# Bias loads over two iterations, shared-block copies on ScalarE, token weights pinned behind the attention

## The chip, the cores and the metric

The kernel runs on one core of a Trainium2 chip. The metric is the device time of one execution in microseconds, as the median of several runs. Five engines work side by side, each through its own instruction queue in order: TensorE (PE, with weight loads as PEld), VectorE (DVE), ScalarE (ACT), GpSimd (POOL) and SyncE (SP). In this kernel SP issues nearly all DMAs.

## The reference, cut to what matters

```python
scores = scale * q @ k.T + bias            # bias[h]: 576 x 576, the same for all 4 batches
attn = softmax(scores); x = attn @ v       # 4 batches, 8 heads, 576 tokens, 64 per head
gate_pre[t] = sum_k conv_w[k] * x[t-4+k]   # 5 taps along the tokens
x = (sigmoid(gate_pre) * (x @ w_val)) @ w_out
theta = x @ w_theta
y = w_tok_r @ (x * cos(theta)) + w_tok_i @ (x * sin(theta))
u = x + y
out = u + relu(u @ w_ch)
```

All inputs are 64-bit floats where they are weights: the kernel fetches the bits of a weight block and makes two 32-bit parts of it (high and low) on the engines.

## The kernel before, in words

**Stages.** First the bias of all heads is computed and stored to scratch in HBM (0 to about 60 us). Then the attention runs (to about 313 us), then the first module (gate and two products, to about 424 us), then the second (theta, the token product, the channel product).

**The attention** has 16 iterations: 4 pairs of heads, and for each pair 4 batches (`self.iters`). An iteration has 5 units `qt` 0 to 4: four blocks of 128 query tokens and a last one in which the 64 left tokens of both heads share one tile. One *step* `s` of the loop in `attention` works at once on three units: scores and softmax of unit `s` (`qk`, `soft`: a DVE instruction at L256 that adds the bias and takes the maximum, then the exponential on ACT at L259), the normalisation on POOL of unit `s-1` (`norm`), the transposes on PE of unit `s-2` (`tr`, `tr_mid`) with their copies out of PSUM (`tr_out`, `mid_out`, through `copy`, L279 on ACT and L281 on DVE), and products with v (`av_ops`, L358). The order of all these is written out by hand: the loop runs under `tc.manual_schedule()`, and each engine gets them in program order. "Shared blocks" are the transposes of `tr_mid` and the last unit: blocks in which two heads share a tile. `mid_out` copies them (tile `em`) on DVE; a letter pair in `EV` says which engine makes the two copies of `tr_out`.

**Beside it** run other pieces, also in that order. `load_bias(p, qt)` fetches the bias of a pair: for `qt` 0 to 3 two DMAs of 288 KB each into one of six `bias` slots (a pair takes four), for `qt` 4 two of 144 KB into one of two `biast` slots. Before, all five are issued in the five steps of the last batch of the pair ahead. `load_qkv(it + 2)` is issued in step 4 of each iteration. `WS` spreads the weight blocks of `w_val`, `w_out`, the convolution and `w_theta`: a block's fetch (`raw`) is issued at the end of step 2, ACT reads it first (L82) at the end of step 4 of the same iteration, and seven more stages follow over two iterations (DVE at L85, L91, L96, L101, then ACT L105 and POOL L108). In the last 16 steps hooks add the first chunk of the convolution, 20 DVE instructions (L469, L478), one a step.

**What the framework orders.** All that is traced outside the manual part is ordered by the framework: it puts each instruction where, by its own estimate, its engine is free, also among the attention's, and the compiled queues then run in that order. So it does with the nine blocks of token weights (`tokblock`, the same eight stages, with two `raw` slots and one `f64h` slot), which `pace` traces between the instructions of the first module, and with `prep`, the convolution of the next chunk. In the trace the fetches of the first three token blocks are issued at 249.5, 266.3 and 278.3 us, inside the attention.

**The first module** works on 8 chunks of 288 tokens: products with `w_val` (48 matmuls a chunk), the gate (`m1_gate`, DVE L509, then a high part on ACT at L63 and a low part on POOL at L65), products with `w_out` of the chunk before. The PSUM of its `gs` tiles and its `mm` tiles lies over that of the attention.

Of the kernel before, what the change touches and what calls it, by code (L numbers as in the profile page):

```python
# [13 lines left out]
AF = mybir.ActivationFunctionType  # L14
# [104 lines left out]
class Kernel:  # L119
# [124 lines left out]
    def soft(self, u, e):  # L244
        nc = self.nc
        it, qt = self.units[u]
        p, _ = self.iters[it]
        if e == 0:
            self.sh[it, qt] = (self.sm_p.tile([128, 2], F32, tag="sm", name="sm"),
                               self.e_p.tile([128, 2 * S], F32, tag="e", name="e"),  # L250
                               self.sm_p.tile([128, 2], F32, tag="mx", name="mx"))
        sm, et, mx = self.sh[it, qt]
        bt = self.bias_t[p, qt]
        ns = self.ns_p.tile([128, 2, HALF], F32, tag="ns", name="ns")
        bb = bt[:, e] if qt < 4 else bt
        nc.vector.tensor_tensor_reduce(  # L256
            out=ns, in0=self.s4[e][:, :, :HALF], in1=bb.rearrange("p (n j) -> p n j", n=2),
            op0=ALU.add, op1=ALU.min, scale=-0.125, scalar=BIG, accum_out=mx[:, e:e + 1])
        nc.scalar.activation(out=et[:, S * e:S * e + S], in_=ns.rearrange("p n j -> p (n j)"), func=AF.Exp,  # L259
                             scale=-1.0, bias=mx[:, e:e + 1], accum_out=sm[:, e:e + 1])  # L260

    def norm(self, u):
        nc = self.nc
# [52 lines left out]

    EV = ["ad", "ad", "aa", "ad", "ad"]

    def mid_out(self, u):
        qt = self.units[u][1]  # L320
        if qt not in (1, 4):
            return
        _, dst, _ = self.ets_dst(u)
        self.copy("d", dst[:, :256], self.po[0][:, 256:512])
        if qt == 4:
            for h in range(2):
                r = slice(64 * h, 64 * h + 64)
                self.copy("d", dst[r, 256:320], self.po[1][r, 384 + 64 * h:448 + 64 * h])

    def tr_out(self, u, eng):  # L330
        qt = self.units[u][1]
        dst, _, o = self.ets_dst(u)
        pt = self.pt[u]
        for h in range(2):
            if self.EV[qt][h] == eng:
                if qt < 4:
                    self.copy(eng, dst[:, o // 64 + h].rearrange("p k q -> p (k q)"), pt[h])
                else:
                    self.copy(eng, dst[:, 4, 4 * h:4 * h + 4].rearrange("p k q -> p (k q)"), pt[h][:, :256])

    def av_ops(self, it, ch):
        nc = self.nc
        p, b = self.iters[it]
        N = 256 + TT * ch
        et, em = self.ets.pop((it, ch))
        vm = self.qkv[it][2]
        po = self.po[ch]
        if ch == 0:
            self.xst[it] = self.xs_p.tile([128, S], F32, tag="xst", name="xst")
        xst = self.xst[it]  # L350

        def step(kb):
            for e in range(2):
                r = slice(64 * e, 64 * e + 64)
                out, rhs = po[r, :N], em[:, :N]
                if kb < 4:
                    out, rhs = out.rearrange("p (h q) -> p h q", q=64), et[:, :N // 64, 4 * e + kb]
                nc.tensor.matmul(out=out, lhsT=vm[:, kb, r], rhs=rhs, start=(kb == 0), stop=(kb == 4))  # L358

        def done():  # L360
            nc.scalar.activation(out=xst[:, 256 * ch:256 * ch + N], in_=po[:, :N], func=AF.Copy)
            if ch == 1:
                nc.sync.dma_start(out=self.x1d[b][:, p, :], in_=xst)

        return [lambda kb=kb: step(kb) for kb in range(5)] + [done]

# [1 line left out]

    WS = ((2, 0, 5, 2), (2, 1, 6, 2), (2, 2, 7, 2), (0, 2, 0, 2), (0, 4, 1, 2), (1, 2, 2, 1), (1, 4, 3, 0),
          (1, 4, 4, 1))  # L370

    AV = {2: (1, 1), 3: (0, 2), 4: (0, 3), 0: (1, 2), 1: (1, 2)}

    def attention(self, blocks, hooks):
# [5 lines left out]
        for s in range(NU + LT + 2):  # L380
# [2 lines left out]
            n = 0 if s >= NU else 2 if r < 4 else 1  # L383
            if s < NU:
                p, b = self.iters[it]
                if b == B - 1 and p + 1 < NP:
                    self.load_bias(p + 1, r)
                for e in range(2):
                    self.qk(s, e)
                if r == 4 and it + 2 < NI:  # L390
                    self.load_qkv(it + 2)
# [308 lines left out]
    def run(self):  # L700
# [11 lines left out]
        with ExitStack() as top:  # L712
# [15 lines left out]
            with ExitStack() as att:  # L728
# [5 lines left out]
                self.e_p = pool(att, "a_e", cfg["EB"], "right", **T)  # L734
                self.sm_p = pool(att, "a_sm", 6, "right", **T)
                blocks, hooks = [], {}
                attention = self.attention(blocks, hooks)
                ps_s = pool(att, "a_ps", 1, space=PSUM, **T)
                self.s4 = [ps_s.tile([128, 2, 512], F32, name=f"s{e}") for e in range(2)]
# [82 lines left out]
            with ExitStack() as m1:  # L822
# [7 lines left out]
                def pace():  # L830
                    slots[0] += 1
                    while todo and (total - len(todo)) * cfg["PC"] < slots[0] * total:
                        todo.pop(0)()

                def prep(c, m):
                    self.m1_conv(c, m)
                    self.m1_sig(c, m)

                NCH = 2 * B
                for c in range(NCH + 1):  # L840
                    for m in range(KC):
# [2 lines left out]
                        elif c < NCH:  # L844
                            self.m1_val(c, m)
                        if c + 1 < NCH:
                            prep(c + 1, m)
                        pace()
                    for m in range(KC):
                        if c == NCH and m in cfg["TH"]:  # L850
# [126 lines left out]
```

## Time and profile before

| | us |
|---|---|
| median of 3 runs | 646.0 (644.36 to 648.67) |
| the profiled execution | 651.17 |
| its span, first to last instruction | 649.4 |
| PE busy in it | 615.2 (95%) |
| DVE busy | 467.3 (72%) |
| ACT busy | 393.4 (61%) |
| POOL busy | 344.5 (53%) |

The mean granted TensorE clock is 0.978 of full speed. Busy shares are means over stages that differ, so the stages are read one by one below. "Busy" of PE is modelled: where it is full, PE is fed without a pause. Iterations of the attention are cut at the DVE instruction that reads a `biast` tile, once an iteration, or, to the same 0.1 us, at the issue of the next q load.

### The profile page before, as it was taken

To read this page: it belongs to the slowest core of one execution; us is meant where nothing else is said; L and a number is where in the kernel's file an instruction comes from. 1 tells how busy PE (TensorE), PEld (TensorE's weight loads), DVE (VectorE), ACT (ScalarE), POOL (GpSimd) and SP (SyncE) were. 2 spreads that over 40 slices of the span, in tenths; PEclk is the share of its full clock that TensorE was granted. 3 is DMA by queue.
4 is the path that set the end of the run, shared out by engine and by line. 5 is a ranking of instruction groups with operands and counts; after the bars stand their busy time and mean duration, and the time that the engine had idled before them with its cause. 6 is when DMAs were issued, how large, how long until landed. Compare 5 with 4: busy or idle time off the path is not lost.

```text
span 649.4 us, 14576 instructions
## 1 busy us (share of the span) xinstructions
PE 615.2 (95%) x5472; PEld 473.2 (73%) x5472; DVE 467.3 (72%) x1089; ACT 393.4 (61%) x851; POOL 344.5 (53%) x422
## 2 busy tenths in 40 slices
PE   6997999999999999989499999999999999999997
PEld 2333555555555555546399999988998999899997
DVE  7995788888887889976579999089987717516212
ACT  5995688788787877656457775388544613613010
POOL 5553567677676666656558875334484324025120
PEclk9998799999999999979799999999999999999999
DMA  7997549755964794431035661623224001200102
GB/s 184 304 312 206 157 127 229 203 150 165 259 177 128 190 256 130 141 92 56 19 110 158 213 173 49 236 70 98 66 74 153 18 1 69 79 1 28 46 1 73
DMA packets 49413, 84.39 MB, mean 130 GB/s; under 512 B 6960, under 2 KB 27568, under 8 KB 48832
## 3 DMA queue, kind: packets, MB, share of 16 engines
q1 hardware_dynamic: 49168, 83.12, 43.9%
q8 instruction: 43, 0.70, 0.5%
q10 hardware_dynamic: 144, 0.30, 0.1%
q14 instruction: 26, 0.21, 0.1%
q0 software_dynamic: 32, 0.07, 0.0%
HBM read 58.39 MB, written 25.07 MB: 129 GB/s over the span
## 4 chain that ended last, share of the span: by engine, by line
PE 74%; DMA 9%; DVE 6%; ACT 4%; POOL 3%; issue 2%; SPq 0%; DVEq 0%; ACTq 0%; POOLq 0%
PE mm L114 15%; PE mm L116 15%; PE mm L115 15%; PE o L358 8%; PE s L242 7%; PE bp L177 5%; PE t L301 4%; DMA bias<-scr 2%; DMA raw<-in_w_val 2%; DMA raw<-in_w_theta 2%; DVE ns L256 2%; POOL e L271 1%; DMA scr<-ev 1%; PE o L313 1%; DMA qr<-in_q 1%
## 5 line engine op out<-in xcount | busy, mean ns | idle before, releaser
L271 POOL TENSOR_SCALAR e<-e,ri 128x576 f32<-128x576 f32 x144 | 116.5, 819 | 58.4 <-DVE ri L269 44.9
L259 ACT ACTIVATE e<-ns,mx 128x576 f32<-128x576 f32 x144 | 111.4, 774 | 35.1 <-DVE mx L256 28.7
L256 DVE CUSTOM_DVE_ANT_0 ns<-s,bias 128x576 f32<-128x576 f32 x128 | 92.1, 752 | 11.9 <-PE s L242 8.4
L242 PE MATMUL s<-kr,qr 64*128 64x288 f32 (+1 forms) x640 | 96.2, 437 | 1.9 <-DVE mx L256 1.9
L116 PE MATMUL mm<-wtok,zl 128*128 128x288 f32 x288 | 84.7, 295 | 0.8 <-POOL zl L65 0.8
L114 PE MATMUL mm<-wtok,zh 128*128 128x288 f32 x288 | 84.7, 295 | 0.0
L115 PE MATMUL mm<-wtok,zh 128*128 128x288 f32 x288 | 84.6, 294 | 0.0
L301 PEld LDWEIGHTS t<-idt,e 64*128 64x128 f32 x1152 | 44.0, 141 | 47.2 <-issue 23.2
L358 PE MATMUL o<-et,vm 128*64 128x320 f32 (+1 forms) x512 | 76.9, 422 | 0.9 <-DVE em L281 0.7
L65 POOL TENSOR_TENSOR ul<-x,uh 128x288 fp32r<-128x288 f32 x32 | 26.8, 837 | 89.3 <-ACT uh L63 68.9
L301 PE MATMUL t<-idt,e 64*128 64x64 f32 x1152 | 55.9, 233 | 9.5 <-POOL e L271 4.7
L279 ACT ACTIVATE et<-t 128x512 f32<-128x512 f32 x96 | 51.6, 554 | 20.0 <-PE t L301 17.7
L242 PEld LDWEIGHTS s<-kr,qr 64*128 64x128 f32 (+1 forms) x640 | 49.8, 183 | 18.2 <-issue 6.2
L625 DVE TENSOR_TENSOR x<-mm,x 128x288 f32<-128x288 f32 x32 | 14.5, 454 | 63.4 <-PE mm L116 63.3
L358 PEld LDWEIGHTS o<-et,vm 128*64 128x64 f32 x512 | 31.8, 137 | 38.1 <-issue 19.3
L478 DVE SCALAR_TENSOR_TENSOR gs<-qr,cw,gs 128x288 f32<-128x288 f32 (+3 forms) x112 | 52.4, 511 | 8.1 <-ACT gs L474 8.1
L63 ACT ACTIVATE uh<-x 128x288 fp32r<-128x288 f32 x32 | 14.1, 441 | 68.3 <-DVE x L625 68.3
L116 PEld LDWEIGHTS mm<-wtok,zl 128*128 128x128 f32 x288 | 54.0, 188 | 1.0 <-POOL zl L65 1.0
L114 PEld LDWEIGHTS mm<-wtok,zh 128*128 128x128 f32 x288 | 54.0, 188 | 0.1
L115 PEld LDWEIGHTS mm<-wtok,zh 128*128 128x128 f32 x288 | 54.0, 188 | 0.1
L281 DVE COPY et<-t 128x512 f32<-128x512 f32 x64 | 39.6, 619 | 18.1 <-PE t L301 14.3
L177 PE MATMUL bp<-h,w2n 128*32 128x512 f32 (+48 forms) x648 | 44.3, 407 | 4.3 <-ACT ev L187 2.3
(123 smaller groups left out, 1569.5 us busy)
## 6 DMA issues: line engine op xcount, KB each, us to landing
scr<-ev SPq DMA_DIRECT2D x36, 296.0 KB, 4.9
qr<-in_q SPq DMA_DIRECT2D x32, 288.0 KB, 4.5
bias<-scr SPq DMA_DIRECT2D x32, 288.0 KB, 8.3
vm<-in_v SPq DMA_DIRECT2D x16, 320.0 KB, 5.5
kr<-in_k SPq DMA_DIRECT2D x16, 288.0 KB, 5.1
x1d<-xst SPq DMA_DIRECT2D x16, 288.0 KB, 4.5
x2d<-xo SPq DMA_DIRECT2D x8, 576.0 KB, 4.1
x<-x2d SPq DMA_DIRECT2D x4, 1152.0 KB, 6.2
```

What stands on the lines that cost most here:

```text
L114: nc.tensor.matmul(out=out, lhsT=wh, rhs=xh, start=first, stop=False)
L115: nc.tensor.matmul(out=out, lhsT=wh, rhs=xl, start=False, stop=False)
L116: nc.tensor.matmul(out=out, lhsT=wl, rhs=xh, start=False, stop=last)
L177: nc.tensor.matmul(out=ps[32 * c:32 * c + 32, n, o:o + hi - lo], lhsT=self.w2n, rhs=rhs, start=True, stop=True)
L242: nc.tensor.matmul(out=out, lhsT=w, rhs=k[r, e], start=True, stop=True)
L256: nc.vector.tensor_tensor_reduce(out=ns, in0=self.s4[e][:, :, :HALF], in1=bb.rearrange("p (n j) -> p n j", n=2), op0=ALU.add, op1=ALU.min, ...
L259: nc.scalar.activation(out=et[:, S * e:S * e + S], in_=ns.rearrange("p n j -> p (n j)"), func=AF.Exp, scale=-1.0, bias=mx[:, e:e + 1], acc ...
L271: nc.gpsimd.tensor_scalar(out=et[:, S * e:S * e + S], in0=et[:, S * e:S * e + S], scalar1=ri[:, e:e + 1], scalar2=1.0, op0=ALU.mult, op1=A ...
L279: self.nc.scalar.activation(out=out, in_=in_, func=AF.Copy)
L301: self.nc.tensor.transpose(out=pt[h][:, 64 * kb:64 * kb + 64], in_=et[r, c:c + 128], identity=self.idt[r, r])
L358: nc.tensor.matmul(out=out, lhsT=vm[:, kb, r], rhs=rhs, start=(kb == 0), stop=(kb == 4))
L478: nc.vector.scalar_tensor_tensor(out=s[:, o:], in0=x[:, o + k:HALF + k], scalar=self.cw[:, m, k:k + 1], in1=s[:, o:], op0=ALU.mult, op1=AL ...
```

## The change

The bias fetch follows a table, `BL`: of the pair ahead, blocks 0, 1 and 4 are issued in steps 1, 3 and 4 of batch 2, and blocks 2 and 3 in steps 1 and 3 of batch 3. From unit 62 on (the last 18), `mid_out` copies with ACT, and `tr_out` uses `EVT`, which gives both copies of units 1 and 4 to ACT. Each instruction of a token block, and of `prep`, is queued behind the last softmax instruction of the attention on DVE and on ACT; the token blocks' fetches also behind the last store of the attention on SP. `tc.issue_after(ins)` only sets the order in the queue of the engine of `ins`; it adds no semaphore.

```diff
     def mid_out(self, u):
...
-        self.copy("d", dst[:, :256], self.po[0][:, 256:512])
+        eng = "d" if u < self.taps_from else "a"
+        self.copy(eng, dst[:, :256], self.po[0][:, 256:512])
         if qt == 4:
             for h in range(2):
                 r = slice(64 * h, 64 * h + 64)
-                self.copy("d", dst[r, 256:320], self.po[1][r, 384 + 64 * h:448 + 64 * h])
+                self.copy(eng, dst[r, 256:320], self.po[1][r, 384 + 64 * h:448 + 64 * h])
...
     EV = ["ad", "ad", "aa", "ad", "ad"]
+    EVT = ["ad", "aa", "aa", "ad", "aa"]
...
-            if self.EV[qt][h] == eng:
+            if (self.EV if u < self.taps_from else self.EVT)[qt][h] == eng:
...
+    BL = {(B - 2, 1): 0, (B - 2, 3): 1, (B - 2, 4): 4, (B - 1, 1): 2, (B - 1, 3): 3}
...
-                if b == B - 1 and p + 1 < NP:
-                    self.load_bias(p + 1, r)
+                if p + 1 < NP and (b, r) in self.BL:
+                    self.load_bias(p + 1, self.BL[b, r])
...
+                self.taps_from = len(self.units) - 18
...
-                        todo.pop(0)()
+                        with tc.issue_after(self.last_d), tc.issue_after(self.last_a), tc.issue_after(self.last_s):
+                            todo.pop(0)()
...
                         if c + 1 < NCH:
-                            prep(c + 1, m)
+                            with tc.issue_after(self.last_d), tc.issue_after(self.last_a):
+                                prep(c + 1, m)
```

`self.last_d`, `self.last_a` and `self.last_s` are set at L256, L259 and L363 to the last instruction traced there.

## Rows read from the trace of the kernel before

**Rows 1.** The page, engines: busy us, share of the span, instructions.
```profile
PE 615.2 (95%) x5472; PEld 473.2 (73%) x5472; DVE 467.3 (72%) x1089; ACT 393.4 (61%) x851; POOL 344.5 (53%) x422
```

**Rows 2.** Windows of four iterations: length; busy per engine; PE clock, DMA share, GB/s.
```profile
199.90:214.22 14.32, 14.32 (x159) 8.28 (x160) 11.32 (x37) 11.40 (x28) 8.50 (x16) 1.00 0.47 144
112.52:127.79 15.27, 14.45 (x159) 8.36 (x161) 12.46 (x36) 11.73 (x29) 10.23 (x16) 1.00 0.81 219
170.81:185.53 14.72, 14.46 (x159) 8.39 (x160) 12.42 (x36) 11.73 (x29) 10.24 (x16) 1.00 0.76 191
228.54:243.85 15.31, 14.46 (x159) 8.40 (x159) 12.48 (x37) 11.74 (x29) 10.25 (x16) 1.00 0.97 252
```

**Rows 3.** Timeline of the SP queue, third bias fetch: start, us, line, tile, count.
```profile
218.45 2.78 SPq L220 DMA_DIRECT2D bias<-scr  x4
222.30 0.33 SPq L651 DMA_DIRECT2D raw<-in_w_theta  x1
```

**Rows 4.** The chain that ended last, same place: start, us, what.
```profile
222.30 10.92 DMA raw<-in_w_theta
```

**Rows 5.** Waits of ACT, 83.88 to 243.85 us: who for whom, total, times, longest.
```profile
ACT f64a L82 <- DMA raw<-in_w_theta: 2.0, 1, 2.0
```

**Rows 6.** Windows of the last three iterations and of PE's pause behind them.
```profile
243.85:260.66 16.81, 15.70 (x169) 8.81 (x167) 15.87 (x42) 12.57 (x31) 11.76 (x18) 1.00 0.45 129
260.66:279.53 18.87, 15.58 (x171) 8.78 (x165) 17.44 (x44) 11.97 (x28) 12.88 (x18) 1.00 0.42 121
279.53:297.02 17.49, 16.77 (x144) 9.42 (x141) 13.46 (x38) 11.98 (x29) 9.35 (x16) 0.80 0.26 83
...
313.60:321.84 8.24, 0.00 (x0) 0.03 (x1) 5.71 (x14) 4.46 (x11) 5.83 (x7) 0.73 0.09 36
```

**Rows 7.** Waits of all engines, 243.85 to 297.02 us.
```profile
ACT e L259 <- DVE mx L256: 10.1, 11, 1.6
```

**Rows 8.** Timeline of DVE in the last iterations: start, us, line, tiles [idle before].
```profile
254.72 1.34 DVE L85 SCALAR_TENSOR_TENSOR f64a<-f64a,raw 128x512 f32<-128x512 f32 x2
...
275.17 0.46 DVE L91 TENSOR_SCALAR f64h<-f64a 128x576 int32<-128x576 int32 x1 [1.21 <-POOL wth L108]
...
276.30 0.74 DVE L96 SCALAR_TENSOR_TENSOR f64h<-f64a,f64h 128x576 int32<-128x576 int32 x1
277.07 1.18 DVE L101 SCALAR_TENSOR_TENSOR f64h<-raw,f64h 128x576 int32<-128x576 int32 x1
```

**Rows 9.** Groups by shape, ACT, 85 to 228 us: busy us, mean ns.
```profile
L279 ACT ACTIVATE et<-t 128x512 f32<-128x512 f32 x50 | 28.6, 592 | 10.3 <-PE t L301 10.2
...
L279 ACT ACTIVATE et<-t 128x256 f32<-128x256 f32 x10 | 3.8, 377 | 0.4 <-PE t L301 0.4
```

**Rows 10.** Groups by shape, DVE, 85 to 228 us.
```profile
L281 DVE COPY et<-t 128x512 f32<-128x512 f32 x30 | 20.7, 690 | 7.0 <-PE t L301 6.5
L281 DVE COPY em<-o 128x256 f32<-128x256 f32 x19 | 7.9, 417 | 0.0
...
L281 DVE COPY em<-o 64x64 f32<-64x64 f32 x20 | 4.3, 217 | 0.1
```

**Rows 11.** The chain that ended last, in PE's pause: start, us, what.
```profile
313.49 0.67 ACT wtok L105
...
317.41 3.81 POOL bias L65 x5
```

**Rows 12.** Windows of the first module behind that pause.
```profile
321.84:340.00 18.16, 18.16 (x117) 18.16 (x118) 14.42 (x32) 10.14 (x25) 9.94 (x12) 0.84 0.28 84
...
355.00:405.00 50.00, 50.00 (x379) 50.00 (x378) 49.11 (x99) 34.25 (x85) 36.69 (x36) 1.00 0.52 150
405.00:424.00 19.00, 19.00 (x132) 18.27 (x132) 2.03 (x5) 6.95 (x17) 5.87 (x6) 1.00 0.56 201
```

**Rows 13.** Groups of DVE, 321.84 to 424 us.
```profile
L85 DVE SCALAR_TENSOR_TENSOR f64a<-f64a,raw 128x576 f32<-128x576 f32 x6 | 6.5, 1077 | 0.0
```

**Rows 14.** The tile wtok: instruction, count, ns min/median/max, first to last start.
```profile
L114 PEld LDWEIGHTS mm<-wtok,zh x288: 187/188/192, 447.9 to 632.6; 128*128 128x128 f32 x144
```

More of the change, by code (lines that the diff above doesn't have):

```diff
@@ L255, in soft @@
         bb = bt[:, e] if qt < 4 else bt
-        nc.vector.tensor_tensor_reduce(
+        self.last_d = nc.vector.tensor_tensor_reduce(
             out=ns, in0=self.s4[e][:, :, :HALF], in1=bb.rearrange("p (n j) -> p n j", n=2),
-            op0=ALU.add, op1=ALU.min, scale=-0.125, scalar=BIG, accum_out=mx[:, e:e + 1])
-        nc.scalar.activation(out=et[:, S * e:S * e + S], in_=ns.rearrange("p n j -> p (n j)"), func=AF.Exp,
-                             scale=-1.0, bias=mx[:, e:e + 1], accum_out=sm[:, e:e + 1])
+            op0=ALU.add, op1=ALU.min, scale=-0.125, scalar=BIG, accum_out=mx[:, e:e + 1]).ins
+        self.last_a = nc.scalar.activation(out=et[:, S * e:S * e + S], in_=ns.rearrange("p n j -> p (n j)"), func=AF.Exp,
+                             scale=-1.0, bias=mx[:, e:e + 1], accum_out=sm[:, e:e + 1]).ins
     def norm(self, u):
@@ L362, in done @@
             if ch == 1:
-                nc.sync.dma_start(out=self.x1d[b][:, p, :], in_=xst)
+                self.last_s = nc.sync.dma_start(out=self.x1d[b][:, p, :], in_=xst).ins
         return [lambda kb=kb: step(kb) for kb in range(5)] + [done]
```

## The prediction

> **What bounds the kernel now.** I read the page first: PE is busy for 95% of the span [rows 1], so time can only come from places where PE waits or runs at the half clock. Windows cut at the iterations of the attention show those places. An undisturbed iteration takes 14.32 us with PE busy for all of it [rows 2]: that is PE's own pace, and no engine can make it shorter. Four places are longer. The three iterations in which the next pair's bias is fetched take 15.27, 14.72 and 15.31 us, PE busy for about 14.46 of each [rows 2]: 0.95 + 0.40 + 0.99 = 2.34 us above the pace. The last three iterations take 16.81, 18.87 and 17.49 us [rows 6], together 53.17 against 3 x 14.32 = 42.96, so 10.2 above it. Behind the attention PE stands still for 8.24 us [rows 6]. In the first module PE is never idle [rows 12], but the first 18.16 us there have a mean clock of 0.84 (of the two levels, 1.2 and 2.4 GHz, the lower one for a while), which loses 0.16 x 18.16 = 2.9 us.
>
> In the last three iterations the reader is to see DVE: busy for 15.87 of 16.81 us and 17.44 of 18.87, against some 12 in an undisturbed iteration [rows 2, 6]. ACT waits there for the maximum from DVE, 10.1 us in all [rows 7]. PE is idle for 18.87 - 15.58 = 3.3 us in the middle one, and the next has a mean clock of 0.80 [rows 6]: the pause is paid twice.
>
> **The bias fetch.** It removes nothing and moves eight DMAs of 288 KB and two of 144 KB, 2.6 MB a pair. An undisturbed iteration moves 144 GB/s x 14.32 us = 2.06 MB [rows 2]. Before, 4.7 MB fall on one iteration; at the 252 GB/s of the fullest one [rows 2] that is 18.5 us, more than it lasts. The queue runs over into the next iteration, and a weight block issued behind the bias DMAs lands only after 10.92 us [rows 3, 4], while ACT reads it two steps (5.7 us) after its issue. ACT, in order, stands for 2.0 us at that read [rows 5], with exponentials queued behind it. After, batch 2 has 2.06 + 1.44 = 3.5 MB (13.9 us) and batch 3 has 3.2 MB (12.7 us): each fits into 14.32 us. In front of each weight block then lies one bias block (two DMAs, 590 KB, 2.3 us), issued a step (2.9 us) earlier, so it has about gone by. Block 2 goes into the slot that block 0 of the pair before held, read by the softmax one step earlier; SP may stand until that is done, with only the weight block's issue queued behind it, a step later. All blocks arrive at least five steps before use. Cost bounds: nothing left (gain 2.34), or 0.40 in each of the six iterations that now carry bias, the smallest excess seen with a full fetch (gain nil). The volume fits, so I take 0.1 for each: gain **1.7 us**.
>
> **The last iterations.** Per iteration DVE loses one copy of 128x512 (0.69 us), one of 128x256 in `tr_out` and two in `mid_out` (0.42 each), and two of 64x64 (0.22 each): at most 2.4 us [rows 10], some 2.0 if neighbours overlap at their ends. The pin takes out token-block work. In the trace the first iteration has one L85 of a token block (0.67), the second the stages L91, L96 and L101 (0.46 + 0.74 + 1.18), a wait of 1.21 us ahead of the first of them, and another L85, the last a third L85 [rows 8]. So DVE would be busy for 15.87 - 2.4 - 0.7 = 12.8, 17.44 - 2.4 - 3.1 = 11.9 and 13.46 - 2.4 - 0.7 = 10.4 us, all below 14.32. DVE stops being the bound.
>
> ACT is next. It gains 0.59 + 3 x 0.38 [rows 9] and two 64x64 copies, for which it has no row: between nothing much and the 0.38 of a 128x256 copy; I take 0.2, nearest to the 0.22 on DVE. That is 2.1 us by durations, about 1.7 with overlap, less one L82 of a token block (about 0.7): 12.57, 11.97 and 11.98 [rows 6] become some 13.6, 13.0 and 13.0 us. That is still below 14.32, but ACT runs in order and stands for 14.32 - 11.4 = 2.9 us of an undisturbed iteration [rows 2], and the copies now sit ahead of exponentials. So I don't take the pace itself but 14.9 us an iteration, 44.7 in all: gain **8.5 us** (bounds 6.4, the rival below, and 10.2).
>
> On the price of the copies: a 128x512 copy is 0.59 us on ACT and 0.69 on DVE [rows 9, 10]. The Trainium skill ("ScalarE: Activation LUTs", What ACT_TABLE_LOAD costs) gives an ACTIVATE without pointer operands 186 ns plus 0.833 ns for each element, with 93 ns of overlap back to back. That is 399 and 613 ns for 256 and 512 columns, and the trace agrees within 6%; for the 64-column copy, of which no run here has an ACT row, it makes an estimate of 239 ns, and the sum stays where it is.
>
> **The pause behind the attention.** ACT's L105 of token block 0 stands in the chain there, 0.67 us ahead of the copy from which the convolution of chunk 1 starts [rows 11]; pinned, the block is only fetched then. Gain **0.6 us**. Bounds: POOL's five low parts (3.81 us) [rows 11] are followed by the last gate value; if the freed POOL works off the three of chunk 2 earlier, 2.3 us more come back. If ACT meets the read of token block 0 before its fetch lands, up to some 3 us go. Pinning `prep` costs nothing: its first instruction already comes behind that L105, 16 us after the last softmax instruction of DVE (297.02, where the last window of the attention is cut [rows 6]).
>
> **The first module** takes over what left the attention: three L85, one each of L91, L96 and L101, 4.1 us at the durations of rows 8, and more where POOL works at the same time: L85 has a mean of 1.08 us there [rows 13] against 0.67, so up to 4.1 x 1.08 / 0.67 = 6.6 us. A gain is excluded, since PE has no idle time there. For hiding it: DVE is idle for 3.7 of the first 18.16 us and 17 of the last 19, but for only 0.9 of the 50 us between [rows 12]. Token weights are first used at 448 us [rows 14], some 40 us after DVE has done the last block, so lateness there is covered. With these go three fetches on SP (576 KB each), three L82 (0.7 us) on ACT and, out of the pause, one L105 and one L108; the DMA engines are half idle there, ACT and POOL above a quarter [rows 12], so I cost them at nothing, unless an L82 meets its fetch too early: then the gate's high parts stand behind it on ACT. I take **0.6 us** lost, close to the lower end, since both ends of the stage have room and PE doesn't wait for a gate value there now; the upper end is 6.6 plus one fall of the clock, 2.9.
>
> The longer L85 is seen beside busy POOL [rows 13]. The Trainium skill ("SBUF — State Buffer") speaks against this move here: DVE with two SBUF inputs and GpSimd take a shared port pair in turns, each for a whole instruction. By it each of the six ops could also stand for a whole POOL low part (3.81 / 5 = 0.76 us), 4.1 + 4.6 = 8.7 us; the measured mean gives 6.6, and my sum goes by that.
>
> **Sum.** -1.7 - 8.5 - 0.6 + 0.6 = -10.2 us. The profiled execution (651.2 us, span 649.4) would become 641.0. It lies 5.2 us above the median of the runs, 0.8%, which scales a saving of 10 by less than 0.1; so 646.0 - 10.2 = **635.8 us**.
>
> **Rivals.**
> (a) ACT becomes the bound of the tail: if its in-order pauses stay at 2.4 us on top of 13.6, 13.0 and 13.0 us, the iterations take 16.0, 15.4 and 15.4 = 46.8; with nothing gained in the pause that is 1.7 + 6.4 - 0.6 = 7.5 saved: 638.5. For: ACT rises above 90% load. Against: 10.1 us of its present idle time is waiting for DVE.
> (b) The first module gives it back: the moved DVE work shows in full with one fall of the clock, 6.6 + 2.9: 1.7 + 8.5 + 0.6 - 9.5 = 1.3 saved, 644.7; with the attention-side durations and no fall, 4.1, 6.7 saved. For: DVE at 49.11 of 50 us. Against: the idle time at both ends.
> (c) Slower: the new order puts token stages ahead of gate values in DVE's queue, and PE runs dry chunk after chunk. The lower clock followed pauses of 3.3 and 8.24 us [rows 6, 12], and pauses of about 1 us didn't bring it [rows 2]; so it decides from some 2 to 3 us a pause. Four such pauses cost 4 x (2.5 + 2.9) = 21.6: 10.8 - 21.6 = 11 slower, 657. Against: before, PE never paused there.
> (d) It doesn't do what it says: the tail is held by something that DVE's load hides (POOL's normalisation, the transposes), and only the bias part and the token ops' 1.2 us wait come back: 2 to 3 saved, 643.5.
>
> **How the numbers follow.** Forecast 0.55, (a) 0.14, (b) 0.17, (c) 0.07, (d) 0.07. One per cent, 6.5 us, is about what a measurement of this kernel can tell from no change (three runs spread over 4.3 us). The forecast and (a) are beyond it, as is a little of (b)'s milder form; small parts of the forecast are not: faster 0.66, same 0.27, slower 0.07. The range reaches down to a tail at full pace with 2.3 us from the pause (631) and up over (a), (d) and part of (b): 631 to 644.
>
> **What would show it.** Right: iterations with bias at 14.4 us in batches 2 and 3; no L82 wait of ACT there; the last three at 14.5 to 15.2, at full clock, no token-block line before the last exponential; PE's pause about 7.7 us; PE without idle time from there to 420 us, DVE near full. Wrong would be: ACT at full load with PE waiting for its copies (a); PE waits for L509 or L65 in the first module, with a clock below 1 ((b), (c)); the last three iterations still at 16 us with DVE idle (d).

## The result, and the profile after

The changed kernel takes 642.27 us (median of 20 runs, 640.48 to 645.23) against 647.69 us (20 runs, 644.36 to 651.21) beside it: ratio 0.9917, 95% interval 0.9898 to 0.9935, 4.2 to 6.6 us saved. A second set gave 642.17 against 649.03 us, ratio 0.9874 (0.9843 to 0.9905), 6.2 to 10.2 us saved. The medians differ by 5.4 and 6.9 us; 6.2 to 6.6 us lies in both intervals. The forecast was 10.2 us, to 635.8: right in sign, too large in size.

The page of the profile after (642.17 us, span 640.4), engines, answers to [rows 1]:

```profile
PE 610.1 (95%) x5472; PEld 470.6 (73%) x5472; DVE 460.4 (72%) x1067; ACT 400.0 (62%) x873; POOL 341.9 (53%) x422
```

The edit moves line numbers: L358, L361, L474, L478 and L509 of the kernel before are L361, L364, L479, L483 and L514 here.

Windows of the kernel after, columns as in [rows 2]. First the three iterations that were stretched by the bias fetch, then the last three, the end of the attention, PE's pause, and three stretches of the first module that answer to [rows 6, 12]:

```profile
111.58:125.90 14.32, 14.32 (x159) 8.27 (x159) 12.59 (x37) 11.89 (x29) 10.48 (x17) 1.00 0.50 145
168.93:183.24 14.31, 14.31 (x159) 8.28 (x159) 12.57 (x36) 11.87 (x29) 10.48 (x17) 1.00 0.40 110
226.20:240.52 14.32, 14.32 (x159) 8.28 (x160) 12.59 (x36) 11.89 (x29) 10.48 (x17) 1.00 0.58 175
240.52:256.05 15.53, 14.40 (x159) 8.29 (x160) 13.40 (x36) 12.48 (x33) 10.53 (x16) 1.00 0.34 98
256.05:271.77 15.72, 14.48 (x159) 8.28 (x159) 12.52 (x33) 13.20 (x35) 10.51 (x18) 1.00 0.37 108
271.77:286.61 14.84, 14.39 (x159) 8.28 (x159) 10.41 (x31) 13.28 (x36) 9.75 (x17) 1.00 0.19 61
286.61:303.64 17.03, 15.06 (x135) 11.01 (x133) 4.12 (x10) 10.33 (x31) 8.53 (x14) 1.00 0.18 54
303.64:313.46 9.82, 0.00 (x0) 0.00 (x0) 7.65 (x17) 5.30 (x13) 5.83 (x7) 0.71 0.43 150
313.46:331.62 18.16, 18.16 (x121) 18.16 (x122) 17.62 (x35) 11.40 (x27) 11.23 (x12) 0.88 0.39 128
346.62:396.62 50.00, 50.00 (x379) 50.00 (x378) 49.08 (x100) 34.58 (x85) 34.80 (x35) 1.00 0.50 153
396.62:415.62 19.00, 19.00 (x131) 18.13 (x130) 2.87 (x7) 6.53 (x15) 5.88 (x6) 1.00 0.52 189
```

The bias iterations run at PE's pace. The last three come down from 53.17 to 46.09 us, but PE still stands for 2.8 us in them. About half of that gain is the clock's: the third ran at a mean clock of 0.80 for 17.49 us [rows 6], a loss of some 3.5 us (0.20 x 17.49), and runs at 1.00 now. The pause became longer. In the first module PE never waits although DVE has more to do (17.62 of the first 18.16 us, against 14.42), so that forecast cost didn't come.

Waits in the last three iterations (240.52 to 286.61 us), answering to [rows 7]: who for whom, total, times, longest.

```profile
...
ACT e L259 <- DVE mx L256: 5.9, 8, 1.2
PEld o L361 <- ACT em L279: 4.2, 3, 1.7
...
PE o L361 <- ACT em L279: 2.8, 3, 1.2
```

The new line is PE waiting for `em`, the copies of the shared blocks (`mid_out`) that the change gave to ACT. The chain that ended last shows one such wait (start, us, what):

```profile
248.72 0.67 ACT e L259 x2
249.39 0.45 ACT em L279 x2
249.84 0.01 issue
249.85 0.23 ACT em L279
250.08 0.04 issue
250.12 1.30 PE o L361 x8
```

Copies stand behind an exponential in ACT's order, and the matmuls that end an output block stand behind the copies. ACT is not full there: it is busy for 12.48 of 15.53, 13.20 of 15.72 and 13.28 of 14.84 us. The same view in the pause answers to [rows 11]:

```profile
303.64 0.44 ACT xst L364
304.07 0.83 ACT gs L479 x2
304.90 0.03 issue
304.93 1.79 DVE gs L483 x4
306.72 0.37 DVE gv L514
307.09 0.02 issue
307.12 0.45 ACT bias L63
307.57 0.07 issue
307.63 5.30 POOL bias L65 x6
312.93 0.02 issue
312.96 0.46 DVE gv L514
```

L105 has left the chain, as forecast: from the start of the store copy to the first `gs` it is 0.43 us, not 1.01. But POOL has six low parts (5.30 us) ahead of the last gate value instead of five (3.81), and DVE four taps (1.79 us) instead of three (1.37). Together -0.58 + 1.49 + 0.42 and some -0.2 for the gate value and the gaps give +1.13: PE stands from 303.64 to 313.46, 9.82 us, against 313.15 to 321.84, 8.69 us, before. (The 8.24 of [rows 6] is a window cut 0.45 later.) Of the 1.49 us of POOL, only about 0.8 are the fourth low part of chunk 2. The rest is length: four of the six take 0.79 to 0.80 us, as all five before, and two take 1.32 and 1.00. They are the two beside which DVE runs token stages, L85 (1.06 us, against 0.74 in the attention) and L91. e12, the same kernel again, has 1.31 and 1.00 there.

**One cut for all runs.** For every profile below: the excess over 14.32 us of the three stretched iterations; the last three iterations; the end, to the start of the last store copy `xst`; the pause, to the first matmul of the first module; the module, to the first use of a token weight as in [rows 14]. Times are medians (number of runs).

| run | excess | three | end | pause | module | us | ratio |
|---|---|---|---|---|---|---|---|
| before | 2.35 | 53.17 | 16.13 | 8.69 | 126.06 | 647.69 (20) | |
| after | 0 | 46.09 | 17.03 | 9.82 | 125.54 | 642.27 (20) | 0.9917 |
| e1 before again | 0.75 | 52.80 | 15.91 | 8.69 | 126.13 | 648.42 (1) | |
| e12 after again | 0 | 46.09 | 17.02 | 9.83 | 125.05 | 642.17 (6) | 0.9874 |
| e2 bias only | 0 | 53.01 | 15.90 | 8.69 | 126.24 | 646.71 (12) | 0.9990 |
| e3 copies only | 2.49 | 51.63 | 18.56 | 8.58 | 126.00 | 649.88 (12) | 1.0021 |
| e4 pins only | 2.96 | 46.64 | 15.90 | 9.96 | 125.90 | 644.17 (10) | 0.9943 |
| e9 no copies | 0 | 46.62 | 15.89 | 9.95 | 125.89 | 642.20 (6) | 0.9870 |
| e5 em copies on DVE | 0 | 44.84 | 16.49 | 9.96 | 125.64 | 640.78 (6) | 0.9886 |
| e6 late stages pinned | 2.26 | 47.66 | 18.85 | 8.69 | 126.11 | 647.04 (12) | 0.9985 |
| e13 the same, further back | 1.28 | 47.73 | 15.90 | 8.58 | 124.82 | 643.48 (6) | 0.9905 |
| e7 gates first | 0 | 46.06 | 17.02 | 2.93 | 130.91 | 640.34 (6) | 0.9885 |
| e8 with e5, 3 buffers | 0 | 44.84 | 16.50 | 2.18 | 132.31 | 638.47 (6) | 0.9859 |
| e10 tokens 1 chunk later | 0 | 44.83 | 18.02 | 2.19 | 132.12 | 639.37 (6) | 0.9835 |
| e11 1.5 chunks later | 0 | 44.83 | 16.50 | 2.18 | 133.90 | 643.27 (6) | 0.9882 |
| e16 from chunk 3 | 0 | 44.81 | 17.99 | 2.18 | 134.13 | 642.42 (6) | 0.9885 |
| e14 from chunk 5 | 0 | 44.80 | 16.49 | 2.18 | 130.28 | 636.18 (1) | |
| e15 the same, timed | 0 | 44.81 | 18.03 | 2.18 | 129.45 | 638.82 (6) | 0.9824 |

Each ratio is against runs of the kernel before on the same chip, whose medians went from 646.85 to 649.47 us; kernels of different sets are best compared by their own medians (e12, the changed kernel again, has the median of the first set, but 0.9874 where 0.990 to 0.994 was expected).

### The profile page after: what moved, and what is told of

Read it like the earlier page. It is cut to its first block, busy times and chain, and to the rows that moved or that the text cites. A ratio compares the mean times of both kernels' runs of the same rounds, so it can differ in the third digit from the quotient of the medians.

```text
span 640.4 us, 14566 instructions
## 1 busy us (share of the span) xinstructions
PE 610.1 (95%) x5472; PEld 470.6 (73%) x5472; DVE 460.4 (72%) x1067; ACT 400.0 (62%) x873; POOL 341.9 (53%) x422
## 4 chain that ended last, share of the span: by engine, by line
PE 83%; ACT 5%; DVE 5%; DMA 2%; issue 2%; POOL 2%; SPq 0%; DVEq 0%; ACTq 0%; POOLq 0%
PE mm L114 16%; PE mm L116 16%; PE mm L115 15%; PE o L361 12%; PE s L242 10%; PE t L301 7%; PE bp L177 4%; PE o L313 2%; ACT e L259 1%; DMA scr<-ev 1%; ACT ev L187 1%; DVE ns L256 1%; PE mm L585 1%; POOL bias L65 1%; DMA bias<-scr 1%
## 5 line engine op out<-in xcount | busy, mean ns | idle before, releaser
L271 POOL TENSOR_SCALAR e<-e,ri 128x576 f32<-128x576 f32 x144 | 114.6, 806 | 57.3 <-DVE ri L269 33.7
L259 ACT ACTIVATE e<-ns,mx 128x576 f32<-128x576 f32 x144 | 111.4, 774 | 27.2 <-DVE mx L256 24.7
L256 DVE CUSTOM_DVE_ANT_0 ns<-s,bias 128x576 f32<-128x576 f32 x128 | 91.9, 752 | 9.6 <-PE s L242 7.0
L242 PE MATMUL s<-kr,qr 64*128 64x288 f32 (+1 forms) x640 | 93.8, 430 | 1.0 <-DVE mx L256 1.0
L361 PE MATMUL o<-et,vm 128*64 128x320 f32 (+1 forms) x512 | 76.9, 422 | 2.8 <-ACT em L279 2.8
L279 ACT ACTIVATE et<-t 128x512 f32<-128x512 f32 (+1 forms) x103 | 54.3, 550 | 20.8 <-PE t L301 18.3
L361 PEld LDWEIGHTS o<-et,vm 128*64 128x64 f32 x512 | 31.4, 137 | 40.0 <-issue 17.6
L483 DVE SCALAR_TENSOR_TENSOR gs<-qr,cw,gs 128x288 f32<-128x288 f32 (+4 forms) x112 | 52.6, 511 | 11.3 <-ACT gs L479 11.3
L281 DVE COPY et<-t 128x512 f32<-128x512 f32 (+1 forms) x57 | 36.1, 634 | 19.9 <-PE t L301 15.6
```

The lines of the kernel that those rows point to most:

```text
L242: nc.tensor.matmul(out=out, lhsT=w, rhs=k[r, e], start=True, stop=True)
L256: self.last_d = nc.vector.tensor_tensor_reduce(out=ns, in0=self.s4[e][:, :, :HALF], in1=bb.rearrange("p (n j) -> p n j", n=2), op0=ALU.add ...
L259: self.last_a = nc.scalar.activation(out=et[:, S * e:S * e + S], in_=ns.rearrange("p n j -> p (n j)"), func=AF.Exp, scale=-1.0, bias=mx[:, ...
L271: nc.gpsimd.tensor_scalar(out=et[:, S * e:S * e + S], in0=et[:, S * e:S * e + S], scalar1=ri[:, e:e + 1], scalar2=1.0, op0=ALU.mult, op1=A ...
L279: self.nc.scalar.activation(out=out, in_=in_, func=AF.Copy)
L483: nc.vector.scalar_tensor_tensor(out=s[:, o:], in0=x[:, o + k:HALF + k], scalar=self.cw[:, m, k:k + 1], in1=s[:, o:], op0=ALU.mult, op1=AL ...
```

## The experiments

**The parts alone.** e1 is the kernel before again; e2 to e4 hold one part of the change each.

```diff
 e2: - taps_from = len(units) - 18    + taps_from = len(units)     (no copies);  no issue_after
 e3: - BL                             + if b == B - 1: load_bias(p + 1, r);      no issue_after
 e4: - BL, - taps_from                  both issue_after kept
```

> The kernel before, once more. My theory: the profiled execution of before (651.2 us) had in its last three iterations a fall of the TensorE clock (290 to 297 us) that most executions lack, and this is why its span is 9.0 us above that of the kernel after while the medians differ by 5.4. Then this profile shows a span of 644 to 647 us, no half clock inside the attention's tail, and the last three iterations some 3 us shorter together (about 50 instead of 53.2). Rival: the tail is the same in all executions and the difference lies elsewhere (start, second module): then 16.8, 18.9 and 17.5 us come again.

> Only the table BL, none of the copies, no pins. My theory: the three transition iterations go from 15.27, 14.72 and 15.31 to 14.32 us each, as in the kernel after, and the time falls by 2.3 us (ratio 0.9964); the tail is that of before. Rival: the time that the bias loads cost is noise of one execution, ratio 1.000.

> Only the copies on ScalarE (EVT and mid_out), old bias loads, no pins. My theory: DVE loses some 2.2 us an iteration in the tail, so the last three iterations come down to about 15.5, 16.5 and 15 us; PE waits some 1.1 us an iteration for the em copies, which stand behind an exponential on ACT; time 3 us lower (ratio 0.995). Rival: the pins did the work, the copies only move load from DVE to ACT: tail at 16 us or more, ratio 0.999 to 1.001.

> Only the pins, old bias loads, copies on DVE. My theory: token stages are gone from the tail, the middle one of the last three iterations falls from 18.9 to about 15.7 us and the others to some 16; PE's pause behind the attention grows from 8.2 to some 9.5 us, because token stages now stand between the gate values and POOL works off chunk 2 first; time 2 to 3 us lower (ratio 0.996). Rival: the pause is as long as before and the lengthening in the kernel after comes from the copies.

e1 refutes the idea that one execution's fall of the clock made the tail look long: its last three iterations take 52.80 us, with a fall in the same place (a mean clock of 0.81 in the third). What varies is the excess of the bias iterations, 2.35 us in one execution and 0.75 in the other. Over the six profiles with the old fetch it is 0.75 to 2.96, mean 2.0 us; in the twelve with the new fetch it is nil. e2's ratio of 0.9990 (0.9964 to 1.0017) allows a gain of 2.0 us (0.9969) as well as none. The pins carry the change: 0.9943 (0.9919 to 0.9967), tail and end together 62.54 us against 68.71 in e1. The copies alone gain nothing, 1.0021 (0.9999 to 1.0043), where 0.995 was expected. DVE now waits in e3's tail for token work, which it does not in before and e1. The moved copies stand ahead of that work on ACT: the first two token blocks are read (L82) 5.7 us after their issue there, and 3.7 and 4.3 us after it in the kernel before.

```profile
DVE f64a L85 <- ACT f64a L82: 4.9, 3, 2.3
```

**The copies.** e9 is the changed kernel without its copies; e5 gives only the copies of `mid_out` back to DVE and keeps those of `tr_out` on ACT. Several expectations call the first "the convolution's"; that name is wrong. `em` holds blocks of the attention that two heads share, and the convolution has no part in these copies.

```diff
 e9: -  self.taps_from = len(self.units) - 18
     +  self.taps_from = len(self.units)
 e5: -  eng = "d" if u < self.taps_from else "a"     # mid_out
     +  eng = "d"
```

> The changed kernel, but the convolution's part of the copies (mid_out: two of 128x256 and two of 64x64 an iteration) stays on DVE in the last three iterations; only the two attention copies (tr_out) go to ACT. Theory 1 (in the tail PE waits for copies that stand behind exponentials in ACT's order): the wait of PE for em on ACT, 7 us in the changed kernel, is gone, the last three iterations fall from 46.1 us to 44.5 to 45.5, and the time is 1 to 2 us below the changed kernel, ratio to the kernel before 0.989 to 0.990. Theory 2 (ACT's and DVE's load as such holds the tail, the place of a copy does not matter): DVE takes 1.3 us an iteration back, the last three iterations stay at 46 us, ratio 0.991 to 0.993.

> The changed kernel without its copies part: in the last three iterations all copies stay on the engines that they had before; bias fetch and pins as changed. Theory 1 (the pins alone shorten the tail, and of the copies the attention's part gains about as much as the convolution's part costs): last three iterations and the end together 62 to 63 us against 63.1 in the changed kernel, ratio 0.990 to 0.993, no difference to the changed kernel beside it. Theory 2 (the forecast's: without the copies DVE stays the bound of the tail): three iterations above 47.5 us, 1.5 us or more above the changed kernel.

In e5 PE's wait for `em` is gone, and the last three iterations fall to 44.84 us, what the forecast had taken (44.7). This repeats: the seven profiles with e5's edit have 44.80 to 44.84 us, the three with both kinds of copies moved (after, e12, e7) 46.06 to 46.09. Windows of e5:

```profile
239.07:254.43 15.36, 15.12 (x165) 8.51 (x166) 14.36 (x40) 12.60 (x32) 11.14 (x17) 1.00 0.33 99
254.43:269.40 14.97, 14.52 (x161) 8.29 (x161) 13.85 (x38) 11.86 (x29) 10.75 (x17) 1.00 0.39 113
269.40:283.91 14.51, 14.06 (x157) 8.19 (x155) 11.62 (x35) 11.95 (x30) 10.10 (x18) 1.00 0.20 63
283.91:300.40 16.49, 14.86 (x135) 10.93 (x131) 4.89 (x14) 9.01 (x26) 8.33 (x13) 1.00 0.18 56
```

DVE is busier than in the changed kernel (14.36 against 13.40 us in the first) and the iteration is shorter: the place of the copy matters, not the load. Tail and end: 62.51 us with no copy moved (e9), 61.33 with those of `tr_out` (e5), 63.12 with both (after). The copies of `tr_out` gain 1.2 us, those of `mid_out` cost 1.8, and the copies as a whole change no median (e9 642.20, e12 642.17 in one set). Only the profiles show e5's 1.8 us; the intervals are wider.

**Which token work held the tail.** e6 is the kernel before with the token stages from L91 on pinned behind the last softmax; fetches, L82 and the three L85 stay. e13 anchors the same stages further back, at the attention's last copy on DVE and last store copy on ACT.

```diff
 e6:  +  if (total - len(todo)) % 8 >= 3:      # L91 and later
      +      with tc.issue_after(self.last_d), tc.issue_after(self.last_a):
      +          todo.pop(0)()
 e13: +  self.last_d = self.nc.vector.tensor_copy(out=out, in_=in_).ins       # copy()
      +  self.last_a = nc.scalar.activation(out=xst[...], ...).ins       # done()
```

> The kernel before, with only one thing moved behind the attention: the token block's stages from L91 on (L91, L96, L101, L105, L108). The fetches, L82 and the three L85 stay in the last iterations; bias fetch and copies as before. Theory 1 (the damage in the tail was a DVE instruction standing in order for POOL or ACT, ahead of a maximum): L91's wait of 1.2 us is gone, and most of what the pins alone gave comes: last three iterations 48 to 50 us, 3 to 5 us saved, ratio 0.993 to 0.995. Theory 2 (it was the sum of DVE's load, or the L85 that wait for L82): the last three iterations stay at 51.5 to 53 us, ratio 0.998 to 1.000.

> The kernel before, with the token stages from L91 on queued behind the last copy of the attention on DVE and its last store copy on ACT, not only behind the last softmax; fetches, L82 and the three L85 stay in the last iterations. Theory 1 (L91, L96 and L101, and the wait for POOL ahead of them, are what the tail lost; behind the last softmax they still stood ahead of the end's reciprocals and copies): last three iterations 47 to 49 us as in the run of the late stages before, and the end 16 to 17 us instead of 18.4; 3 to 5 us saved, ratio 0.992 to 0.995, as much as the full pins alone (0.994). Theory 2 (it is the L85 that wait in order for L82): the end stays above 18 us or the iterations come back above 51; ratio 0.997 to 1.000.

In e6 the iterations gain 5.1 us over e1, as theory 1 has it, but the end loses 2.9 and the median is that of before, the number of theory 2. DVE's timeline there (start, us, line, tiles, idle before) tells why:

```profile
290.42 0.45 DVE L91 TENSOR_SCALAR f64h<-f64a 128x576 int32<-128x576 int32 x1
291.86 0.17 DVE L269 RECIPROCAL ri<-sm 128x2 f32<-128x2 f32 x1 [0.98 <-POOL sm L268]
...
292.99 1.18 DVE L101 SCALAR_TENSOR_TENSOR f64h<-raw,f64h 128x576 int32<-128x576 int32 x1
295.90 0.16 DVE L269 RECIPROCAL ri<-sm 128x1 f32<-128x1 f32 x1 [1.73 <-POOL sm L268]
```

The pin let the stages go directly behind the last softmax, among the reciprocals of the end. That window has a clock of 0.91 in e6, and 1.00 in e13, which takes 15.90 us there. PE is busy for 16.30 us in the one and 14.77 in the other, and idle for 2.55 and 1.13: of the 2.95 us, 1.5 are the clock's and 1.4 waiting. Whether the order brought the fall of the clock is open, as the last section has two executions of one kernel that differ by such a fall alone. e13 puts the stages behind the copies, and the iterations keep their gain (47.73 us). Its ratio, 0.9905 (0.9874 to 0.9936), is as good as the whole change.

So L91, L96 and L101 of one token block, 2.4 us of work with a wait of 1.21 us in front [rows 8], held most of the tail. In the kernel before they lie on the chain that ended last, seen from 270 to 285 us (start, us, what):

```profile
276.38 0.67 DVE f64h L96
277.05 0.02 issue
277.07 1.18 DVE f64h L101
278.25 0.60 DVE et L281
```

PE waits 1.58, 0.93 and 0.72 us between 276.1 and 280.3 us, and from 279.9 us its clock is the lower one. In the four profiles with that chain in the tail (before, e1, e2, e3) the clock falls in the third iteration, in the other fourteen it doesn't. The third iteration in e13:

```profile
278.07:292.70 14.63, 14.05 (x155) 8.06 (x151) 12.29 (x37) 11.71 (x29) 10.20 (x18) 1.00 0.20 62
```

Of the 5.1 us between e1 and e13, some 3.3 are that clock (0.19 x 17.12 us). The fetches, L82 and the three L85 are worth another 1.1 us of the iterations (47.73 to 46.64 in e4). But this comes back: from the last three iterations to the end of the module e13 takes 197.0 us, the pins alone 198.4, the whole change 198.5 and 198.0 (e12). Holding back L91 and what follows was enough.

**The pause.** e7 puts the four gate values of the first chunk first, and chunk 1's convolution, the token stages and chunk 2's low parts behind the last of them. e8 adds e5's edit and a third gate buffer. e10, e11, e16 and e14 (e15 is the same kernel, timed) are e8 with the token stages starting later: after 8, 12, 24 and 40 of 56 slots. Line numbers of these kernels are one higher.

```diff
 e7:  +  if c == 0:
      +      for m in range(KC): self.m1_gate(c, m)
      +      self.last_d, self.last_a, self.last_p = self.gate_ins
      +  with tc.issue_after(self.last_p):
             self.m1_split(c + 2, m)
 e8:  +  gv = self.f_p.tile([128, HALF], F32, tag="gv", name="gv", bufs=3)
 e10: -  (total - len(todo)) * cfg["PC"] < slots[0] * total
      +  slots[0] > 8 and (total - len(todo)) * (cfg["PC"] - 8) < (slots[0] - 8) * total
```

> The changed kernel, but in the pause behind the attention all four gate values of the first chunk come first in the queues: the preparation of chunk 1, the token stages and the low parts of chunk 2 are queued behind the last gate's instructions on DVE, ACT and POOL. Theory 1 (the pause of 9.9 us is POOL's four low parts of chunk 2 ahead of the low part that frees the gate buffer, and the token stages between): pause 3 to 5 us, 5 to 7 us below the changed kernel, ratio 0.981 to 0.985. Theory 2 (the pause is the drain of the attention itself, its last copies and the PSUM that they free): pause stays above 8 us, ratio 0.990 to 0.993; or what was held back is missing later, and PE waits in the first module for chunk 1, with the same total.

> Both together (the convolution's copies on DVE, the gates first), and a third buffer for the gate value. Theory 1 for both: pause 2 to 4 us, last three iterations 44.5 to 45.5 us, ratio 0.977 to 0.983, the fastest of all. Theory 2 for both: as the changed kernel, 0.990 to 0.993.

> As the kernel with the gates first, three gate buffers and the convolution's copies on DVE, and the token stages start one chunk later in the first module (the same number of slots less eight, the same end). Theory 1 (the pauses of PE in the first module there, 8 us of waits, come from ACT, which stands in order for the fetch of a token block, 4.1 us, ahead of the convolution of chunk 1): they fall to 0 to 3 us and the time to 630 to 634 us, ratio 0.975 to 0.981. Theory 2 (DVE's own work for chunks 1 and 2 is what was put off and is late): waits stay at 6 to 8 us, ratio 0.984 to 0.988.

> The same with the token stages starting one and a half chunks later. Theory 1: as the one before or up to 1 us better, ratio 0.974 to 0.981; the token work, pressed into less time, may take a gate value's place in DVE's order later. Theory 2: 0.984 to 0.988.

> The changed kernel again, unchanged, beside the others of this set. Every theory: ratio 0.990 to 0.994; no clock or excess of one execution to explain: the iterations with a bias fetch at 14.3 us, the last three and the end at 62.5 to 63.5 us, the pause 9.8 to 10.0 us.

> The kernel with the gates first, three gate buffers and the convolution's copies on DVE, and no token stage before chunk 5 of the first module, so that the second module waits for token weights and the time as a whole tells nothing. Read are PE's waits in the first 75 us of the first module, 8 us or so in the runs with the token stages there. Theory 1 (DVE with POOL has more to do than PE there because of the token stages moved into it): the waits fall to 0 to 2 us. Theory 2 (the convolution's own work, put off from the pause, is late whatever the token stages do): 5 to 9 us of waits remain.

> The kernel with the token stages last, as in the single look before it (636.2 us), now timed. If the waits that token stages made in the first chunks are really gone and not only moved: 634 to 637 us, ratio 0.979 to 0.983, below the changed kernel and below the kernel with the gates first alone (0.986). If they only moved behind chunk 5: 638 to 640 us, ratio 0.985 to 0.988.

> The same with the token stages from chunk 3 of the first module on, spread over 32 slots in place of 16. If what matters is that DVE is ahead before the token stages come: waits of PE there 1 to 3 us in all, ratio 0.979 to 0.984. If the token stages cost PE the same wherever they stand in a module without a pause: waits 4 to 6 us, 0.985 to 0.988.

The pause does come from the order: it falls to 2.93 us in e7 and 2.18 in e8. But of e7's 6.9 us the first module takes 5.4 back, and the median falls by 1.9; e8 is at 0.9859, above the 0.977 to 0.983 expected. PE, which never waited there, now does (e7, then e8, from the end of the pause to 437 us, without the wait that is the pause itself):

```profile
PE mm L116 <- POOL bias L65: 2.9, 2, 2.0
PE mm L115 <- ACT xo L529: 0.2, 1, 0.2
```

```profile
PE mm L115 <- ACT xo L529: 2.6, 2, 2.3
PE mm L116 <- POOL bias L65: 2.2, 2, 1.8
PE mm L115 <- DVE gv L515: 0.4, 1, 0.4
```

That is 3.1 us in e7 and 5.2 in e8; the 8 us that the expectations of e10 and e14 name count the pause as well. About 1.1 us more of e7's 5.4 are the clock's (0.91 and 0.92 over the first 18.16 us and the next 21.35, against 0.88 over the first 18.16 alone in the changed kernel), and the rest stays open. In the chain that leads to e7's longest wait (it ends at 331.56 us) a token block's fetch comes early, with ACT standing in order:

```profile
303.45 4.09 DMA raw<-in_w_tr
307.53 0.02 issue
307.56 0.76 ACT f64a L83
```

e10 and e11 were to cure that by starting the token stages later; they didn't: pause and module together stay at 134.3 and 136.1 us (e8 134.5, after 135.4). With the tokens from chunk 5 (e14) PE has no wait between the pause and 345 us and 1.6 us before 380, so the stages do cause the early waits. They cause others later. Windows of e15: the pause, then up to 380 us, then to the first use of token weights:

```profile
305.27:307.45 2.18, 0.00 (x0) 0.00 (x0) 0.46 (x1) 1.45 (x5) 1.33 (x2) 1.00 0.43 140
307.45:380.00 72.55, 72.55 (x546) 72.55 (x547) 64.25 (x136) 49.85 (x124) 49.92 (x54) 1.00 0.48 149
380.00:436.90 56.90, 52.19 (x304) 45.47 (x303) 46.47 (x79) 37.82 (x75) 26.14 (x21) 1.00 0.48 152
```

72.55 us without a gap, then 4.7 us of idle PE behind the point where the tokens start. Pause and module together: 131.6 us, 3.7 less than in the changed kernel. e16 (136.3) shows that an earlier start with more slots is no better: PE waits 7.3 us there, more than either of its theories gave. DVE has 7.65 us of work in the changed kernel's pause, most of it for later chunks: what the pause loses in PE's time, it gives in advance work. Of 7.6 us that e15 takes out of it, 3.9 come back.

e8 and e15, 638.47 and 638.82 us, ratios 0.9859 (0.9816 to 0.9901) and 0.9824 (0.9789 to 0.9859), beat both kernels: all six executions of e15 and five of e8's lie below all 26 of the changed kernel. Between e8, e10 (0.9835, 0.9799 to 0.9871) and e15 the intervals show no difference.

## Why the prediction was wrong in its size

Each term against two pairs of executions (after minus before, and e12 minus e1), in us:

| term | forecast | after - before | e12 - e1 |
|---|---|---|---|
| bias fetch | -1.7 | -2.35 | -0.75 |
| last three iterations | -8.5 | -7.08 | -6.71 |
| end of the attention | 0 | +0.90 | +1.11 |
| pause | -0.6 | +1.13 | +1.14 |
| first module | +0.6 | -0.52 | -1.08 |
| elsewhere | 0 | -1.1 | -1.1 |
| span | -10.2 | -9.0 | -7.4 |

**The bias fetch: right.** With a mean excess of 2.0 us over six profiles, 1.7 was a good value; all iterations that carry bias now run at the pace, and ACT has no wait at L82 there (before, 2.0 us at one such read [rows 5]).

**The last iterations: mis-sized, the largest error.** Three iterations and the end were to save 8.5 us and saved 6.2 (5.6 in the second pair). The step that failed is the one that took 14.9 us an iteration: DVE and ACT both came out under 14.32 by load, and only 0.6 us was added for copies ahead of exponentials on ACT; the iterations took 15.4. It asked what the moved copies would hold up on ACT, and not who waits for the copies: PE, for `em`, 2.8 us. Rival (a) had such a wait among its signs, and 46.8 us for the three; 46.09 was measured, and e5 without that wait gives 44.84. But (a) laid it on ACT at full load, and ACT was not full: the copies' place in its order made the wait. The end was counted as untouched, though the copies run into it: 17.03 us against 15.89 without them (e9). And the credit was wrongly shared: I laid the gain on 2.4 us of copies an iteration, but it is the token work's, mostly one chain that stands in order (e4, e13), and the fall of the clock behind it. That "the pause is paid twice" was right, though the 3.3 us are not one pause: the longest of its gaps are 1.58 and 0.93 us.

The 64-column copies were costed at 0.2 us and take 0.216 (mean of 8). The Trainium skill ("ScalarE: Activation LUTs", What ACT_TABLE_LOAD costs) gives the formula from which the estimate of 239 ns came, 11% more; the size of a copy was never the trouble.

**The pause: wrong sign.** L105 left the chain and gave its 0.58 us. The upper bound, "if the freed POOL works off the three of chunk 2 earlier", went the other way: POOL has four of chunk 2's low parts and two of the gate's in the chain. e4, with the pins alone, has the longer pause too (9.96 us). What I missed is that the pins bring token stages in between the gate values: L82 on ACT, L85 and L91 on DVE, beside which two of POOL's low parts take 1.32 and 1.00 us instead of 0.79. That adds about 0.7 us, and the fourth part of chunk 2 about 0.8. The order of POOL is the framework's; that the new place of the token stages made it put this part ahead is likely, but not shown. Together with the sign of the forecast the term is off by 1.7 us.

**The first module: right.** It costs nothing, as the idle time at its ends takes the moved work. The 0.5 and 1.1 us by which it is shorter are the clock's: its first 18.16 us run at 0.88 and 0.90 instead of 0.84 in both executions before, since more of the stretch at the lower clock lies in the longer pause. L85 lasts 0.99 us on average there (8 of them), and that length reaches no matmul of the module. The Trainium skill ("SBUF — State Buffer", SBUF: two separate sides) has DVE, with two SBUF inputs, and GpSimd take a shared port pair in turns. The trace agrees as far as the durations go: three L85 of a token block take 0.74 us in the attention, and of the eight here four take 0.75 and four 0.88 to 1.82. By the price of that rule the moved work could take 8.7 us; the idle time hid whatever it took. Two slips in the forecast's bound cancel: the 0.67 us were read from a row that mixes two shapes (a token block's L85 takes 0.74), and three L85, L91, L96 and L101 add up to 4.6 us, not 4.1; 4.6 x 1.08 / 0.74 is 6.7, against 6.6. But this cover hangs on the pause: once the pause is cut, PE waits for token work wherever it is put (e7 to e16). Rivals (b) and (c) had that mechanism; in the changed kernel it didn't set in.

**The base.** The forecast subtracted savings read from one execution, 651.2 us, from a median of 646.0 that later runs put at 647.7 (20 runs); of the 6.5 us between 635.8 and 642.27, 1.7 are that. Part of what the profiled execution had over others lay in the very iterations that the change repairs, but the excess taken (2.35 us) is close to its mean (2.0). With that mean for the bias and the second pair's terms for the rest, the parts that the change touches save 7.5 us; the two sets of medians say 5.4 and 6.9. That difference stays open. The 1.1 us "elsewhere" lie at the kernel's start, which no edit touches: the first read of a `biast` tile comes at 65.9 to 70.2 us in the profiles, and from the first use of a token weight on all four executions take 201.4 to 201.5 us.

## What to carry to other kernels

Before a step goes to an engine with room, ask who waits for its result and what stands ahead of it in that engine's order; reckoned from load, with 0.6 us added, an iteration came to 14.9 us, and the copies' place made it 15.4. A short chain of another job that waits in order (2.4 us of token work) cost this tail some 5 us, 3.3 of them through the lower clock that followed its pauses. Moving it is worth doing alone, as long as its new place is behind the last instruction that anything waits for, and moving the rest with it gained nothing more here. A pause of the bounding engine can be the time in which the others get ahead: look at what they do in it before counting it as a gain, and take a saving's size from several executions.

## What the runs showed of the hardware that I had not expected

A pause of 9.82 us is followed by 18.16 us at a mean granted clock of 0.88. One of 2.18 us is followed by 72.55 us at 1.00 in e15, and by 18.16 us at 0.91 in e16, though PE is fed without a gap in both; so the length of a pause, from which rival (c) reckoned, does not decide alone. e14 and e15 are one kernel; the end of the attention took 16.49 us at a clock of 1.00 in the one profile and 18.03 at 0.91 in the other, with DVE (6.16 and 6.17 us), ACT and POOL equally busy and PE's longest wait the same (1.3 us). A fall of the clock can so come and go between executions with no edit, at 1.5 us. Of e15's six executions, five have a mean clock of 0.988 or 0.989 over the whole kernel; the one with 0.995, as in e14, is the fastest (636.30 us). The excess of one iteration under a full bias fetch also goes from nothing (the third in e1) to 1.5 us (the third in e4) between executions of kernels with that same fetch.

In the pause of the changed kernel two token stages on DVE and the POOL parts beside them are longer on both engines: L85 1.06 us instead of 0.74 beside a part of 1.32 instead of 0.79, and L91 0.63 instead of 0.46 beside one of 1.00. In e12 all four are the same within 0.02 us. No run took the token stages alone out of that pause, so it is not shown that the one lengthens the other.
